# Batch 0 in two token parts, v cast by its transfer, and output stores on the ScalarE queue, in an attention + squared-ReLU kernel on one Trainium2 core

## The chip, the cores and the metric

The kernel runs on one core of one Trainium2 chip. Time is microseconds (us) of device time, a median of several executions. In this kernel TensorE (PE in the profile) does matrix multiplies, VectorE (DVE) and ScalarE (ACT) work on vectors, GpSimd (POOL) casts and issues casting transfers, SyncE (SP) issues most other transfers. With a run of the kernel before in the same call, the ratio is the mean time of one kernel's fast runs over that of the other's fast runs of the same rounds. It is therefore not quite the ratio of the medians that are quoted. The interval after a ratio is a 95% interval.

## The reference

```python
# q, k, v: (8, 8, 576, 64); beacon_k, beacon_v: (8, 8, 16, 64); all float32
k_all = concat([beacon_k, k], axis=2); v_all = concat([beacon_v, v], axis=2)
scores = q @ k_all.T / sqrt(64)              # causal, the 16 beacon keys are always seen
a = softmax(scores)
x = (a @ v_all).transpose(0, 2, 1, 3).reshape(4608, 512)
h = x @ w_in                                 # (512, 2048)
out = maximum(h, 0) ** 2 @ w_out             # (2048, 512) -> (4608, 512)
```

## The kernel before

A small list scheduler inside the kernel fixes the order of instructions on each engine. Each operation has an engine, a priority, dependencies and an *estimated* duration. The scheduler simulates time with the estimates and always issues the ready operation of the best priority. The program then holds each engine's list in that fixed order.

The chain is this. The attention of batch `b` ends with the attention-value matmuls ("av"). VectorE normalizes them into `xn`. SyncE issues five transposing transfers `xT <- xn`. The MLP goes through the tokens in chunks of 512. Its first multiply ("s1", with `w_in`), for the chunk that needs batch `b`, reads `xT`. Its second multiply gives two output units of 256 tokens for each chunk. On the same SyncE queue stand loads of q, k and v for later batches, the transposing transfers `qT` and `kT` of batch `b+2`, and the output stores.

```python
# staging load (SyncE), later cast by GpSimd
ld = add(f"ld{b}{x}{c}", "POOL" if soft else "SP", 1.3 if lo else 0.65, emit_load, prio=prio,
         take=("stg", "stg"), dma=1.1 * rows / 128, behind=load_chain[-1:] + behind, sync=sync)
# zero padding of the q/k area, once batches 1 and 2 are transposed (GpSimd)
deps = trans[NPE - 1, "q"] + trans[NPE - 1, "k"] + trans[NPE - 2, "q"] + trans[NPE - 2, "k"]
zero_ops[b] = add(f"zero{b}", "POOL", 1.0, emit, prio=10.0 * b - 1, deps=deps)
# qT / kT by transposing transfer (SyncE), batches 3 to 7
trans[b, x] = [add(f"tr{b}{x}", "SP", 3.8, emit, prio=prio, deps=deps, dma=3.2)]
# scores (TensorE): 0.17 is the fixed part of the estimate
qk = add(f"qk{p}.{n}.{i}", "PE", 0.17 + cols / 2400.0, emit_qk, prio=base + i, ...)
# xT of one 128-token tile (SyncE), batches 2 to 7; batches 0 and 1 are transposed by TensorE
deps = [norm_ops[HP * b + i, 0] for i in range(HP)] + ring_deps(tok, tok + n)
o = add(f"xt{b}.{t}", "SP", 1.32, emit, prio=-50.0 + b, deps=deps, dma=0.64 * n / 128)
# second multiply of the MLP, chunk 0: the two output units u in turn, quarter by quarter
order2 = [(u, [(ts, 4 * qd, 4 * qd + 4) for ts in range(2)], [qd]) for qd in range(4) for u in range(2)]
# output: ScalarE copies PSUM to osb, SyncE stores
ev = add(f"ev{j}.{u}", "ACT", 1.05 if ts is None else 0.6, emit_ev, prio=-15.0, ...)
st_ops[2 * j + u] = add(f"st{j}.{u}", "SP", 0.65, emit_st, prio=-20.0, deps=[ev], dma=1.4)
# filler matmuls that keep TensorE busy while the first data come
def keep_busy(slot, gap):
    for _ in range(int((gap - 0.2) / (0.07 if warm_pe else 0.11))):     # 25 the first time
        nc.tensor.matmul(ps[slot][:, 0, 0:128], filler, filler, start=True, stop=True)
# ... (cuts between all of these)
```

The softmax here doesn't subtract the row's maximum and nothing guards it: scores larger than these inputs give would overflow.

Of the kernel before, what the change touches and what calls it, by code (L numbers as in the profile page):

```python
# [187 lines left out]
def kernel(  # L188
# [11 lines left out]
    nc = tc.nc  # L200
# [9 lines left out]
    NCH = n_tokens // TCH  # L210
    NMC = d_model // 128
# [53 lines left out]
    warm_pe = []  # L265

    def keep_busy(slot, gap):
        for _ in range(int((gap - 0.2) / (0.07 if warm_pe else 0.11))):
            nc.tensor.matmul(ps[slot][:, 0, 0:128], filler, filler, start=True, stop=True)  # L269
        warm_pe.append(slot)  # L270
# [26 lines left out]
    tri_op = add("tri", "POOL", 1.0, emit_tri, prio=-150.0)  # L297
# [28 lines left out]
    SOFT_V = (1,)  # L326
    zero_ops = {}
    strided = {}

    def add_zero(b):  # L330
        def emit(e):
            nc.gpsimd.memset(qb[b % 2][:, :, NT - 1, :], 0.0)
            nc.gpsimd.memset(kb[b % 2][:, :, NT - 1, :], 0.0)
        deps = trans[NPE - 1, "q"] + trans[NPE - 1, "k"] + trans[NPE - 2, "q"] + trans[NPE - 2, "k"]
        zero_ops[b] = add(f"zero{b}", "POOL", 1.0, emit, prio=10.0 * b - 1, deps=deps)

    def add_load(b, x, c, prio, behind=[], sync=[]):
# [6 lines left out]

        soft = b in SOFT_V
        queue = nc.gpsimd if soft else nc.sync

        def emit_load(e):
            st = stg[ld.held[2]]
            insts = []  # L350
            if lo:
                insts.append(queue.dma_start(out=st[0:Nb], in_=beacon[b].transpose([1, 0, 2])))
            insts.append(queue.dma_start(out=st[lo:rows],  # L353
                                         in_=t[b, :, t0:t0 + rows - lo, :].transpose([1, 0, 2])))
            return insts

        ld = add(f"ld{b}{x}{c}", "POOL" if soft else "SP", 1.3 if lo else 0.65, emit_load,
# [14 lines left out]
        if x != "v":  # L372
            if b < NPE + 2:
                deps += [zero_ops[b]]
            else:
                deps += trans[b - 2, x]
        engs = ("POOL", "DVE") if b == 0 else ("POOL",)
        cast[b, x, c] = add(f"cast{b}{x}{c}", engs, {"DVE": 0.6, "POOL": 0.65}, emit_cast,
                            prio=prio, deps=deps, give=ld)

    def add_trans(b, x, prio):
# [11 lines left out]
        trans[b, x] = [add(f"tr{b}{x}", "SP", 3.8, emit, prio=prio, deps=deps, dma=3.2)]  # L393
# [9 lines left out]
    def add_strided(b, prio):  # L403
        loads = {}
        bk = add_beacon(b, prio)
        after = [w_ops["in", 3]] if b == 1 else [strided[b - 1][HP - 1, "q"]] if b else []
        free = trans[b - 2, "q"] + trans[b - 2, "k"] if b >= 2 else []
        trans[b, "q"], trans[b, "k"] = [], []
        step = 1 if b == 0 else 2
        for pr in range(0, HP, step):  # L410
            h = slice(2 * pr, 2 * (pr + step))
            for n, (x, t, dst) in enumerate((("k", k, ks), ("q", q, qs))):
                def emit(e, t=t, dst=dst, h=h):
                    return [nc.gpsimd.dma_start(out=dst[b % 2][:, h],
                                                in_=t[b, h].rearrange("h (p s) d -> p h s d", s=NS))]
                o = add(f"sld{b}{x}{pr}", "POOL", 0.65 * step, emit, prio=prio + pr + 0.1 * n, behind=after,
                        deps=free, dma=0.92 * step)
                for i in range(step):
                    loads[pr + i, x] = o
        strided[b] = loads  # L420
        for pr in range(HP):
# [3 lines left out]
            for part in (("k", "q") if b == 0 else ("kq",)):  # L425
                def emit_tp(e, pr=pr, h=h, boxes=boxes, part=part):
                    pp = ps[boxes[part].held[2]].bitcast(BF16)
                    if "k" in part:
                        nc.tensor.transpose(pp[:, 1, 0:Nb], bks[b % 2][:, h, :], ident[0:Nb, 0:Nb])
                    for x, half, at, t in (("k", 1, Nb, ks), ("q", 0, 0, qs)):  # L430
                        if x in part:
                            for u in range(NS):
                                for hj in range(2):
                                    nc.tensor.transpose(pp[64 * hj:64 * hj + 64, half, at + u * NP:at + (u + 1) * NP],  # L434
                                                        t[b % 2][:, 2 * pr + hj, u, :], ident[0:NP, 0:NP])

                tp = add(f"tp{b}.{pr}{part}", "PE", 0.2 + 0.35 * len(part), emit_tp,
                         prio=100.0 * (HP * b + pr) - 190 + (5 if part == "q" else 0),
                         deps=[bk, ident_op] + [loads[pr, x] for x in part] + busy, take=("ps", "tp"))

                def emit_k(e, pr=pr, boxes=boxes, part=part):
                    pp = ps[boxes[part].held[2]].bitcast(BF16)
                    copy_on(e, kT[b % 2][:, pr, 0:Nb], pp[:, 1, 0:Nb])
                    copy_on(e, kT[b % 2][:, pr, Nb:Nb + S].rearrange("p (n s) -> p n s", s=NS),
                            pp[:, 1, Nb:Nb + S].rearrange("p (s n) -> p n s", s=NS))

                def emit_q(e, pr=pr, boxes=boxes, part=part):
                    pp = ps[boxes[part].held[2]].bitcast(BF16)
                    copy_on(e, qT[b % 2][:, pr, 0:S].rearrange("p (n s) -> p n s", s=NS),
                            pp[:, 0, 0:S].rearrange("p (s n) -> p n s", s=NS))  # L450

                boxes[part] = tp
                ev = []
                if "k" in part:
                    ev.append(add(f"ek{b}.{pr}", "DVE", 0.9, emit_k, prio=-200.0, deps=[tp]))
                    trans[b, "k"].append(ev[-1])
                if "q" in part:
                    ev.append(add(f"eq{b}.{pr}", ("DVE", "ACT") if b else "ACT", 0.75, emit_q, prio=-199.0, deps=[tp]))
                    trans[b, "q"].append(ev[-1])
                add(f"tpg{b}.{pr}{part}", "-", 0.0, None, prio=0.0, deps=ev, give=tp)  # L460
# [48 lines left out]
    def add_pair(b, pr):  # L509
# [8 lines left out]
        if b < NPE:  # L518
            qk_deps = [trans[b, "k"][pr], trans[b, "q"][pr]]
        else:  # L520
            qk_deps = trans[b, "k"] + trans[b, "q"]
        take_pt = add(f"pt{p}", "-", 0.0, None, prio=100.0 * p, deps=qk_deps, take=("pt", "pt"), gate=gate)
        av_ops[p] = []
        for n, ph in enumerate(phases(b)):
            add_phase(b, pr, p, n, ph, take_pt, qk_deps, gate)

    def add_phase(b, pr, p, n, ph, take_pt, qk_deps, gate):
        base = 100.0 * p + 1000.0 * n
        exps = []
        for i in range(0, len(ph.pieces), QGROUP(b)):  # L530
# [17 lines left out]
            qk = add(f"qk{p}.{n}.{i}", "PE", 0.17 + cols / 2400.0, emit_qk, prio=base + i,  # L548
# [12 lines left out]
        def emit_mask(e):  # L561
# [5 lines left out]
            if ph.last is not None:  # L567
# [5 lines left out]
                   prio=base, deps=exps + [tri_op])  # L573
# [96 lines left out]
    def add_weights():  # L670
        for i in range(4):
            def emit(e, i=i):
                w = d_ff // 4
                return [nc.gpsimd.dma_start(
                    out=w_in_sb[:, :, i * w:(i + 1) * w],
                    in_=moe_w_in.rearrange("(m p) f -> p m f", p=128)[:, :, i * w:(i + 1) * w])]
            w_ops["in", i] = add(f"win{i}", "POOL", 1.3, emit, prio=-100 + i, sync=[v_loads[0][2]] if i == 0 else (),
                                 behind=[w_ops["in", i - 1]] if i else (), dma=3.15)
    def add_weights_out():
        for i in range(4):  # L680
# [5 lines left out]
            w_ops["out", i] = add(f"wout{i}", "POOL", 1.3, emit, prio=-90 + i, behind=[v_loads[1][4]] if i == 0 else [w_ops["out", i - 1]], dma=3.15)  # L686

    def add_chunk(j):
# [59 lines left out]
        for n, (u, work, quarters) in enumerate(order2):  # L748
            def emit_s2(e, u=u, work=work):
                o = ps[s2_first[j, u].held[2]]  # L750
                for ts, f0, f1 in work:
# [4 lines left out]
            o = add(f"s2.{j}.{u}.{n}", "PE", 1.73, emit_s2, prio=base + 100 + n,  # L756
                    deps=[x for qd in quarters for f in (2 * qd, 2 * qd + 1) for x in sq[f]]
                    + [w_ops["out", qd] for qd in quarters] + [prevs.get(u)],
                    take=("ps", "mlp") if u not in prevs else None, pe_time=1.73)
            if u not in prevs:  # L760
                s2_first[j, u] = o
            prevs[u] = o
            s2_ops[j, u] = o
        for u in range(2):
            last = j == NCH - 1 and u == 1

            for ts in (range(2) if last else [None]):
                def emit_ev(e, u=u, ts=ts):
                    o = ps[s2_first[j, u].held[2]]
                    d = osb[(2 * j + u) % 2]  # L770
                    if ts is not None:
                        o, d = o[:, ts, :], d[:, ts, :]
                    copy_on(e, d, o)

                deps = [s2_ops[j, u]]
                if (2 * j + u) >= 2:
                    deps.append(st_ops[2 * j + u - 2])
                ev = add(f"ev{j}.{u}", "ACT", 1.05 if ts is None else 0.6, emit_ev, prio=-15.0, deps=deps,
                         give=s2_first[j, u] if ts != 0 else None)

                def emit_st(e, u=u, ts=ts):
                    t0 = j * TCH + u * 256
                    d = osb[(2 * j + u) % 2]
                    if ts is None:
                        nc.sync.dma_start(out=out[t0:t0 + 256, :].rearrange("(t p) d -> p t d", p=128), in_=d)
                    else:
# [82 lines left out]
```

## Time and profile before

| | before |
|---|---|
| time, median of 3 (lowest to highest) | 355.68 us (354.88 to 358.15) |
| TensorE busy | 342.2 of 355.2 us |
| first s1 matmul | 28.2 us |
| waits of TensorE for `xT` | 3.5 us in two waits |
| granted TensorE clock, mean | 0.993 |

The page's first two parts: busy time of the engines, then the span in 40 slices, where each digit is a share in tenths and PEclk is the granted clock of TensorE.

```profile
PE 342.2 (96%) x3037; PEld 183.2 (52%) x3037; DVE 149.5 (42%) x293; ACT 189.6 (53%) x231; POOL 79.8 (22%) x130
...
PE   6999999899999999899997999999999999999994
...
PEclk9999999999999999999998999999999999999999
```

TensorE is busy 96% of the span, and 76% of the page's chain of work that ended last is on it, so it sets the time. The clock row shows one dip after the middle: the clock's records read half from 190.0 to 193.4 us. At the very start the row reads 9, but the trace has no clock record before 22.8 us. The timeline of TensorE (start, duration, what, how many) shows the real state there: twelve 96-column transposes take 0.69 us at 11.8 us, where twenty-four take 0.70 us at 36.1 us, so the clock was half there. The first s1 comes at 28.2 us.

```profile
11.79 0.69 PE L434 MATMUL ps<-ident,qk_area 96*64 96x96 bf16 x12
...
28.22 0.99 PE L713 MATMUL ps<-xT,w_in 128*128 128x240 bf16 x8
```

The waits of TensorE (who waited for what: us in total, times, longest), with one line, and the same two waits in TensorE's timeline (the brackets hold idle time and its releaser):

```profile
PE ps L713 <- DMA xT<-xn: 3.5, 2, 2.4
```

```profile
150.59 1.67 PE L713 MATMUL ps<-xT,w_in 128*128 128x512 bf16 x7 [1.13 <-DMA xT<-xn]
...
189.44 2.19 PE L713 MATMUL ps<-xT,w_in 128*128 128x256 bf16 x12 [2.42 <-DMA xT<-xn]
```

Timelines of VectorE and SyncE around the first of them: the last normalization of batch 3 (the 20th in order: batch 0 has eight, each later batch four), then what SyncE issued until `xT` of batch 3 had its turn.

```profile
132.05 0.82 DVE L601 TENSOR_TENSOR xn<-ps,rcp 128x640 bf16<-128x640 f32 x1
```

### The profile page before, as it was taken

Reading aid. Unit: us, or ns where it says so; the run is one execution under the profiler, and the core shown is the slowest. Engines: PE = TensorE matmul, PEld = TensorE weight load, DVE = VectorE, ACT = ScalarE, POOL = GpSimd, SP = SyncE. Lnnn points to the kernel's source line nnn. Section 1 sums busy time; section 2 is a strip of 40 time slices with the busy share of each in tenths; the row PEclk is TensorE's granted clock in tenths of the full one; section 3 lists DMA queues with packets and bytes.
Section 4 is the critical chain, followed back from the end, with each engine's and each line's share of the span. In section 5 each row is a group of like instructions: output and inputs, shape, how many; then the busy total and the mean of one; then the engine's idle time right before and its main releaser. Section 6 shows DMA issues by size and latency. Waiting matters only on the chain.

```text
span 355.2 us, 7320 instructions
## 1 busy us (share of the span) xinstructions
PE 342.2 (96%) x3037; PEld 183.2 (52%) x3037; DVE 149.5 (42%) x293; ACT 189.6 (53%) x231; POOL 79.8 (22%) x130
## 2 busy tenths in 40 slices
PE   6999999899999999899997999999999999999994
PEld 5569676554444444444444874444444544444441
DVE  4576784546542483236332482247224601401300
ACT  2776786867643754466443753575357305504602
POOL 8254802461422254024131330000000000000000
PEclk9999999999999999999998999999999999999999
DMA  8899999999969999789997994110211123003003
GB/s 138 145 203 216 204 205 207 244 206 214 194 118 216 225 222 234 144 154 241 229 198 138 235 222 86 61 59 18 53 59 61 28 41 118 0 2 118 0 2 118
DMA packets 137010, 49.51 MB, mean 139 GB/s; under 512 B 123344, under 2 KB 132048, under 8 KB 136976
## 3 DMA queue, kind: packets, MB, share of 16 engines
q1 hardware_dynamic: 127472, 40.09, 54.0%
q0 software_dynamic: 9504, 8.95, 15.5%
q8 instruction: 24, 0.39, 0.5%
q14 instruction: 10, 0.08, 0.1%
HBM read 37.22 MB, written 9.44 MB: 131 GB/s over the span
## 4 chain that ended last, share of the span: by engine, by line
PE 76%; DMA 11%; SPq 6%; DVE 2%; ACT 1%; issue 1%; POOL 1%; ACTq 0%; POOLq 0%
PE ps L713 31%; PE ps L753 28%; PE ps L585 7%; PE ps L541 6%; SPq L632 3%; DMA stg<-in_k_dram 3%; DMA stg<-in_q_dram 3%; DMA stg<-in_v_dram 3%; PE ps L434 2%; DMA xT<-xn 1%; DMA qk_area<-in_q_dram 1%; SPq L353 1%; PE ps L269 1%; SPq L385 1%; DVE g L738 1%
## 5 line engine op out<-in xcount | busy, mean ns | idle before, releaser
L713 PE MATMUL ps<-xT,w_in 128*128 128x512 bf16 (+3 forms) x704 | 133.5, 342 | 4.0 <-DMA xT<-xn 3.5
L753 PE MATMUL ps<-w_out,g 128*128 128x512 bf16 x576 | 132.0, 381 | 0.5 <-ACT qT L306 0.5
L555 ACT ACTIVATE pt<-ps 128x832 bf16<-128x832 f32 (+4 forms) x128 | 104.1, 865 | 45.0 <-PE ps L541 44.9
L713 PEld LDWEIGHTS <-w_in 128*128 128x128 bf16 x704 | 66.4, 98 | 60.6 <-issue 4.8
L738 DVE TENSOR_TENSOR g<-g 128x1024 bf16<-128x1024 bf16 (+2 forms) x80 | 52.9, 663 | 104.3 <-ACT g L729 104.0
L729 ACT ACTIVATE g<-ps 128x1024 bf16<-128x1024 f32 (+2 forms) x62 | 59.1, 953 | 61.6 <-PE ps L713 61.6
L753 PEld LDWEIGHTS <-g 128*128 128x128 bf16 x576 | 53.5, 98 | 67.5 <-issue 6.9
L308 POOL CAST qk_area<-stg 128x512 bf16<-128x512 f32 (+2 forms) x50 | 32.5, 658 | 55.0 <-DMA stg<-in_k_dram 32.6
L306 ACT COPY osb<-ps 128x1024 f32<-128x1024 f32 (+1 forms) x19 | 18.3, 968 | 44.0 <-PE ps L753 40.9
L585 PEld LDWEIGHTS <-pt 128*128 128x128 bf16 (+1 forms) x960 | 34.1, 99 | 8.0 <-issue 2.9
L541 PE MATMUL ps<-qT,kT 64*128 64x80 bf16 (+5 forms) x400 | 37.7, 290 | 0.0
L585 PE MATMUL ps<-vb,pt 128*128 128x65 bf16 (+1 forms) x960 | 36.3, 196 | 0.2 <-ACT pt L555 0.2
L308 POOL CAST vb<-stg 128x512 bf16<-128x512 f32 (+1 forms) x36 | 22.3, 638 | 56.4 <-DMA stg<-in_v_dram 33.2
L565 DVE TENSOR_TENSOR pt<-pt,tri 128x1024 bf16<-128x1024 bf16 (+1 forms) x36 | 24.3, 674 | 20.7 <-ACT pt L555 20.6
L601 DVE TENSOR_TENSOR xn<-ps,rcp 128x640 bf16<-128x640 f32 (+2 forms) x36 | 27.0, 750 | 1.8 <-DVE rcp L600 0.5
L600 DVE RECIPROCAL rcp<-ps 128x10 f32<-128x10 f32 (+2 forms) x36 | 7.6, 210 | 43.5 <-PE ps L585 43.5
L541 PEld LDWEIGHTS <-kT 64*128 64x128 bf16 x400 | 12.6, 96 | 20.7 <-issue 16.2
L731 DVE TENSOR_SCALAR g<-ps 128x1024 bf16<-128x1024 f32 (+2 forms) x18 | 19.0, 1054 | 8.1 <-PE ps L713 7.4
L308 DVE COPY kT<-ps 128x16 bf16<-128x16 bf16 (+1 forms) x24 | 9.7, 456 | 8.6 <-PE ps L434 8.0
L434 PE MATMUL ps<-ident,qk_area 96*64 96x96 bf16 x288 | 11.1, 233 | 2.0 <-DMA qk_area<-in_k_dram 1.1
L306 ACT COPY qT<-ps 128x576 bf16<-128x576 bf16 x12 | 7.7, 638 | 8.9 <-PE ps L434 6.2
L434 PEld LDWEIGHTS <-qk_area 96*64 96x64 bf16 x288 | 8.5, 126 | 3.6 <-DMA qk_area<-in_k_dram 1.2
(36 smaller groups left out, 71.3 us busy)
## 6 DMA issues: line engine op xcount, KB each, us to landing
out_dram<-osb SPq DMA_DIRECT2D x17, 512.0 KB, 2.8
stg<-in_v_dram SPq DMA_DIRECT2D x21, 256.0 KB, 5.6
stg<-in_q_dram SPq DMA_DIRECT2D x20, 256.0 KB, 4.8
stg<-in_k_dram SPq DMA_DIRECT2D x15, 256.0 KB, 4.6
w_in<-in_moe_w_in_dram POOLq DMA_DIRECT2D x4, 512.0 KB, 8.6
w_out<-in_moe_w_out_dram POOLq DMA_DIRECT2D x4, 512.0 KB, 10.9
stg<-in_v_dram SPq DMA_DIRECT2D x7, 224.0 KB, 4.5
qk_area<-in_k_dram POOLq DMA_DIRECT2D x4, 288.0 KB, 12.3
```

The costliest lines, as they stand in the source:

```text
L306: nc.scalar.copy(dst, src)
L308: eng[e].tensor_copy(dst, src)
L434: nc.tensor.transpose(pp[64 * hj:64 * hj + 64, half, at + u * NP:at + (u + 1) * NP], t[b % 2][:, 2 * pr + hj, u, :], ident[0:NP, 0:NP])
L541: nc.tensor.matmul(st[:, hj, at:at + t1 - t0], kT[b % 2][hp, pr, 128 * c:128 * c + 128], qT[b % 2][hp, pr, t0:t1], start=True, stop=True,)
L555: nc.scalar.activation(pt[take_pt.held[2]][:, :, off:off + width], st[:, :, 0:width], AF.Exp, bias=0.0, scale=scale)
L565: nc.vector.tensor_tensor(out=d, in0=d, in1=tri[:, m0:m0 + m, :][:, None].to_broadcast([128, 2, m, 128]), op=ALU.min)
L585: nc.tensor.matmul(a[:, hj, (t - tl[0]) * (D + 1):(t - tl[0] + 1) * (D + 1)], P[0:rr, hj, o:o + 128], vb[b % 2][0:rr, c, h, :], start=(c = ...
L601: nc.vector.tensor_tensor(out=xn[b % 2].rearrange("p t (h d) -> p h t d", d=D)[:, 2 * pr:2 * pr + 2, tl[0]:tl[0] + nt], in0=a[:, :, :, 0:D ...
L713: nc.tensor.matmul(h[:, u, lo - spans[0][0]:hi - spans[0][0]], w_in_sb[:, mc, ft * 128:(ft + 1) * 128], xT[:, mc, lo % RING:lo % RING + hi ...
L729: nc.scalar.activation(dst, h, AF.Relu, bias=0.0, scale=1.0)
L738: nc.vector.tensor_tensor(out=d, in0=d, in1=d, op=ALU.mult)
L753: nc.tensor.matmul(o[:, ts, :], G[:, fc, (2 * u + ts) * 128:(2 * u + ts + 1) * 128], w_out_sb[:, fc, :], start=(fc == 0), stop=(fc == NFT ...
```

## The change

The intent: start the MLP earlier, by bringing only 240 of batch 0's 576 tokens first, by moving the first quarter of `w_in` forward, and by casting v of batches 0 and 1 in the transfer instead of in a step of its own behind a staging buffer. More filler matmuls were meant to bring the full TensorE clock before the first transposes (in e11 below, with 50 of them, it was full from 5.1 us and the first transposes came at 5.96). The stores leave the SyncE queue, but for the last two. The last output unit is computed in halves, so that the first half is evicted under the second. Some estimates of the scheduler are changed too. The diff is cut to its core:

```diff
-    warm_pe = []
+    warm_pe, FILL = [], 50
-        for _ in range(int((gap - 0.2) / (0.07 if warm_pe else 0.11))):
+        for _ in range(FILL if not warm_pe else int((gap - 0.2) / 0.07)):
...
+    FIRST = [("kq", 0, 0), ("kq", 0, 2), "tri", ("v", 0, 1), ("kq", 1, 0), ("win", 0), ("kq", 1, 2), ("v", 2, 3, 4),
+             ("win", 1), ("win", 2), ("win", 3)]
+    SPLIT_AT = 240
...
+    def add_v(b, tiles, prio, behind=()):           # batches 0 and 1
+                insts.append(nc.gpsimd.dma_start(out=vb[b % 2][lo:rows, c, :, 0:D],
+                                                 in_=v[b, :, t0:t0 + rows - lo, :].transpose([1, 0, 2])))
...
+    PARTS = {0: [Part(0, SPLIT_AT, 0), Part(SPLIT_AT, S, 1)], 1: [Part(0, S, 1)], 2: [Part(0, S, 0)]}
...
-            qk = add(f"qk{p}.{n}.{i}", "PE", 0.17 + cols / 2400.0, emit_qk, prio=base + i,
+            qk = add(f"qk{p}.{n}.{i}", "PE", 0.2 + cols / 2400.0, emit_qk, prio=base + i,
...
-            o = add(f"s2.{j}.{u}.{n}", "PE", 1.73, emit_s2, prio=base + 100 + n,
+            o = add(f"s2.{j}.{u}.{n}", "PE", 1.75, emit_s2, prio=base + 100 + n,
...
+                    if ts is None:
+                        nc.scalar.copy(d, o)
+                        nc.scalar.dma_start(out=out[t0:t0 + 256, :].rearrange("(t p) d -> p t d", p=128), in_=d)
+                    else:                                 # LAST_U, the last unit, in halves
+                        nc.scalar.copy(d[:, ts, :], o[:, ts, :])
+                        nc.sync.dma_start(out=out[t0:t0 + 128, :], in_=d[:, ts, :])
...
-                st_ops[2 * j + u] = add(f"st{j}.{u}", "SP", 0.65, emit_st, prio=-20.0, deps=[ev], dma=1.4)
+                ev = add(f"ev{j}.{u}", "ACT", 1.15 if ts is None else 0.65, emit_ev, prio=-15.0, deps=deps, give=first)
+                st_ops[2 * j + u] = add(f"st{j}.{u}", "-", 4.0, None, prio=0.0, deps=[ev])
```

## The prediction

> **What bounds the kernel now.** The page shows PE busy 96% of 355.2 us, but not all of it useful. Summing the real matmuls at their start-to-start times late in the trace (216 ns for a 128x512, 29 ns for an attention-value matmul) against time: about 18.6 us of PE time are lost by 30 us, 2 more by 45 us, some 7 in small pieces by 140 us, 5 at 186-193 us, 4.3 after the last matmul. The rest is dense and untouched. So three places to win:
>
> 1. *Start.* The chain of waits opens with the q/k DMA (4.96 us); the first s1 matmul (L713) comes at 28.2 us. Until about 22.8 us PE runs at half speed: in the timeline twelve 96-column transposes take 0.69 us there, twenty-four take 0.70 us at 36 us. [...] the 25 first fillers last 2.85 us, then PE waits for DMA. 50 would last about 5.4 us cold[...].
> 2. *Middle.* SP issues almost without a gap from 75 to 192 us (q/k transposes 3.1-5.2 us each, five xT transposes 6.4-7 us, loads 0.5-1.1 us, stores 0.5-1.4 us), and PE waits for xT 1.13 us at 150 us and 2.42 us at 187 us; after the latter comes a half-clock stretch.
> 3. *Tail.* Two evictions (1.07 us) and two stores after the last matmul.
>
> **What the change does.** The first q/k transfers bring 240 tokens of four heads, so phase 0 of all four pairs, and xT of 240 tokens, need half of batch 0. The first w_in quarter, issued at 15.6 us before, follows the third q/k transfers, about 9-11 us by issue times of 0.64-0.75 us. In the static order s1 starts after 7.2 us of useful PE work instead of 8.9, with phase 1 of pairs 2-3 still open. I expect the first s1 at 18-22 us and the first 240 tokens' s1 done near 30 us (36 before). Limits: ScalarE has about 20 us of exps and copies for batch 0, and the bytes ahead of the last w_in quarter are the same. The casting v transfers read the same 256 B pieces; I cost them like the plain ones, about 5 us a batch. Gain 4-6 us.
>
> Stores leave SP: about 1 us each, two per batch, and no load waits behind an eviction. ScalarE pays about 0.5 us each and has room. Against it: the new PE order puts the last attention-value matmul of batches 3 to 6 only 8.5 us of PE work before the s1 that needs it (17 before). Norm 1.1, three xT transposes 3.9 and landing 2.5 make 7.5 us if SP is free. The middle waits may shrink or move: -1, between -4 and +3.
>
> Tail: the first half is evicted under the second: -0.5 us.
>
> **Prediction: 349.0 us, range 344.5 to 353.5**; faster by over 2% 0.45, within 2% 0.51, slower 0.04.
>
> **Right if:** transposes before 10 us run at full speed; first s1 before 22 us; batch-1 transposes near 31 us (36 before); no store on SP; about 4.0 us after the last matmul. **Wrong if:** the casting v transfers are slow (w_in quarters and batch 1 late), PE falls back to half clock between 7 and 20 us, or new PE waits for xT of 3 us or more appear.

Gains are 4 to 6 us at the start, 1 in the middle and 0.5 at the end, 6.5 us with the mean of the first, which from 355.7 us makes about 349. The 5.4 us for 50 fillers and the 0.5 us for a store on ScalarE were estimates; in the kernel after they are 5.52 us and 0.38 us (median of 17).

## More of the kernel before

```profile
132.11 4.24 SPq L353 DMA_DIRECT2D stg<-in_v_dram  x4
136.46 4.75 SPq L385 DMA_TRANSPOSE qT<-qk_area  x1
141.30 3.39 SPq L385 DMA_TRANSPOSE kT<-qk_area  x1
144.75 0.58 SPq L353 DMA_DIRECT2D stg<-in_v_dram  x1
145.42 6.41 SPq L632 DMA_TRANSPOSE xT<-xn  x5
```

The data for `xT` of batch 3 were ready at 132.87 us, and the transfer was issued at 145.42. For 12.6 us it stood behind other work of the same queue.

## The result

The kernel after takes 371.13 us (370.62 to 372.96, 4 runs) against 355.28 for the kernel before in the same rounds. The ratio is 1.0451, with a 95% interval of 1.0367 to 1.0535. So it is slower, and outside the predicted range of 344.5 to 353.5.

The same views of the kernel after. First the page's busy times and slices:

```profile
PE 346.1 (93%) x3116; PEld 187.5 (51%) x3152; DVE 155.8 (42%) x300; ACT 185.1 (50%) x228; POOL 84.1 (23%) x130
...
PE   8999899999999999279994999999999999999995
...
PEclk9559999999999999769998799999999999999999
```

TensorE now has a hole near 150 to 160 us and another near 200. The clock's records read half from 153.6 to 163.8 us and from 201.4 to 208.2 us, and close to the start from 10.2 to 27.3 us. The waits and the timelines name the hole:

```profile
PE ps L772 <- DMA xT<-xn: 13.5, 2, 9.0
```

```profile
149.33 1.90 PE L814 MATMUL ps<-w_out,g 128*128 128x512 bf16 x8
160.21 3.57 PE L772 MATMUL ps<-xT,w_in 128*128 128x512 bf16 x8 [8.98 <-DMA xT<-xn]
```

```profile
140.91 0.82 DVE L661 TENSOR_TENSOR xn<-ps,rcp 128x640 bf16<-128x640 f32 x1
```

```profile
141.08 5.35 SPq L352 DMA_DIRECT2D stg<-in_v_dram  x4
146.53 4.00 SPq L401 DMA_TRANSPOSE qT<-qk_area  x1
150.63 4.28 SPq L401 DMA_TRANSPOSE kT<-qk_area  x1
155.00 6.45 SPq L692 DMA_TRANSPOSE xT<-xn  x5
```

`xT` of batch 3 was ready to be issued at 141.73 us and was issued at 155.00, 13.3 us later, behind four v loads and the two transposing transfers of batch 5. The queue time is about the same as before (12.6 us). What differs is how much work TensorE had in between. In the static order of before, 17 us of TensorE work lie between the last attention-value matmul and the s1 that needs it. In the order of after it is 8.5 us for most batches and about 10 us for batch 3 (weighed as in the sum below).

The start, in the timeline of TensorE:

```profile
6.62 0.62 PE L461 MATMUL ps<-ident,qk_area 40*64 40x40 bf16 x24
...
9.84 0.59 PE L461 MATMUL ps<-ident,qk_area 40*64 40x40 bf16 x24
10.37 0.49 PE L601 MATMUL ps<-qT,kT 64*128 64x240 bf16 x4
```

Four score matmuls with 240 columns take 0.33 us at 8.2 us and 0.49 us from 10.4 us on. The clock's records say the same: full from 6.8 to 10.2 us, then half until 27.3.

To follow the lost time I made a sum of my own from the trace (not a view of the profile). It is the elapsed time less the dense duration of all matmuls whose weight loads have begun. The dense durations are those seen late in the trace (216 ns for a 128x512, in proportion to columns for narrower ones, 30 ns for an attention-value matmul, 22 ns for a transpose). Fillers count as lost.

| lost TensorE time up to | before | after |
|---|---|---|
| 20 us | 15.4 | 14.0 |
| 35 us | 19.2 | 19.4 |
| 140 us | 28.7 | 29.9 |
| 170 us | 31.2 | 41.5 |
| 210 us | 37.2 | 50.4 |
| 300 us | 40.4 | 54.7 |

The spans differ by 16.0 us (371.2 less 355.2). Of this, 1.2 came by 140 us, 9.1 between 140 and 170, 2.9 between 170 and 210, 1.1 from 210 to 300. The 96 extra transposes cost 2.1 (96 times 22 ns), and the end after the last weight load is 0.3 shorter (4.75 against 5.09 us). The terms add to 16 within rounding.

### The profile page after: what moved, and what is told of

Read it like the earlier page. It is cut to its first block, busy times and chain, and to the rows that moved or that the text cites. A ratio compares the mean times of both kernels' runs of the same rounds, so it can differ in the third digit from the quotient of the medians.

```text
span 371.2 us, 7429 instructions
## 1 busy us (share of the span) xinstructions
PE 346.1 (93%) x3116; PEld 187.5 (51%) x3152; DVE 155.8 (42%) x300; ACT 185.1 (50%) x228; POOL 84.1 (23%) x130
## 4 chain that ended last, share of the span: by engine, by line
PE 75%; DMA 9%; SPq 5%; POOL 4%; DVE 3%; issue 2%; ACT 1%; POOLq 0%; DVEq 0%; ACTq 0%
PE ps L772 30%; PE ps L814 30%; PE ps L645 7%; PE ps L601 6%; DMA stg<-in_q_dram 3%; DMA stg<-in_k_dram 3%; DMA qk_area<-in_k_dram 3%; SPq L692 2%; PE ps L461 1%; SPq L401 1%; POOL vb L310 1%; SPq L352 1%; POOL qk_area L435 1%; DVE g L790 1%; DMA stg<-in_v_dram 1%
## 5 line engine op out<-in xcount | busy, mean ns | idle before, releaser
L772 PE MATMUL ps<-xT,w_in 128*128 128x512 bf16 (+3 forms) x687 | 137.1, 348 | 15.8 <-DMA xT<-xn 13.5
L788 ACT ACTIVATE g<-ps 128x1024 bf16<-128x1024 f32 (+2 forms) x54 | 53.1, 983 | 75.0 <-PE ps L772 74.6
L601 PE MATMUL ps<-qT,kT 64*128 64x80 bf16 (+7 forms) x400 | 37.1, 288 | 0.8 <-DVE kT L310 0.6
L625 DVE TENSOR_TENSOR pt<-pt,tri 128x1024 bf16<-128x1024 bf16 (+1 forms) x36 | 24.5, 681 | 28.2 <-ACT pt L615 28.2
L310 POOL CAST vb<-stg 128x512 bf16<-128x512 f32 (+1 forms) x30 | 19.2, 661 | 72.9 <-DMA stg<-in_v_dram 51.6
L835 ACT COPY osb<-ps 128x1024 f32<-128x1024 f32 x17 | 17.2, 1013 | 36.5 <-PE ps L814 36.5
L790 DVE TENSOR_SCALAR g<-ps 128x1024 bf16<-128x1024 f32 (+2 forms) x26 | 26.0, 1002 | 15.4 <-PE ps L772 13.6
L308 ACT COPY qT<-ps 128x576 bf16<-128x576 bf16 (+2 forms) x16 | 8.2, 519 | 14.7 <-PE ps L461 10.0
L310 DVE COPY kT<-ps 128x16 bf16<-128x16 bf16 (+3 forms) x28 | 10.4, 413 | 10.2 <-PE ps L461 9.3
L461 PE MATMUL ps<-ident,qk_area 96*64 96x96 bf16 (+2 forms) x384 | 11.7, 209 | 0.8 <-DMA qk_area<-in_k_dram 0.8
L461 PEld LDWEIGHTS <-qk_area 96*64 96x64 bf16 (+2 forms) x384 | 9.5, 120 | 2.4 <-DMA qk_area<-in_k_dram 1.3
## 6 DMA issues: line engine op xcount, KB each, us to landing
w_in<-in_moe_w_in_dram POOLq DMA_DIRECT2D x4, 512.0 KB, 12.2
qk_area<-in_k_dram POOLq DMA_DIRECT2D x4, 288.0 KB, 12.6
```

The lines of the kernel that those rows point to most:

```text
L310: eng[e].tensor_copy(dst, src)
L461: nc.tensor.transpose(pp[64 * hj:64 * hj + 64, half, at + u * n:at + (u + 1) * n], t[pt_.i][0:n, 2 * pr + hj, u, :], ident[0:n, 0:n])
L601: nc.tensor.matmul(st[:, hj, at:at + t1 - t0], kT[b % 2][hp, pr, 128 * c:128 * c + 128], qT[b % 2][hp, pr, t0:t1], start=True, stop=True,)
L625: nc.vector.tensor_tensor(out=d, in0=d, in1=tri[:, m0:m0 + m, :][:, None].to_broadcast([128, 2, m, 128]), op=ALU.min)
L772: nc.tensor.matmul(h[:, u, lo - spans[0][0]:hi - spans[0][0]], w_in_sb[:, mc, ft * 128:(ft + 1) * 128], xT[:, mc, lo % RING:lo % RING + hi ...
L788: nc.scalar.activation(dst, h, AF.Relu, bias=0.0, scale=1.0)
```

## The experiments

### First group: the estimate, and a late memset

The static order flips with one number. With the estimate 0.2 for a score group, the scheduler interleaves both output units of chunk 0, which hold two of the four PSUM slots. The last q/k transposes of batch 2 then come late. So does the GpSimd memset of the padding that waits for them: it starts at 80.3 us in the kernel after and at 67.9 us before. Meanwhile SyncE issues nothing for 14.1 us (68.7 to 82.8 in the kernel after): its next load waits for GpSimd's first cast to empty a staging buffer, and that cast comes behind the memset. My first theory was that this late memset delays all later loads, and with them `xT`. The rival was that the start or the stores cause the loss.

**e1: the kernel after with the old estimate.**

```diff
-            qk = add(f"qk{p}.{n}.{i}", "PE", 0.2 + cols / 2400.0, emit_qk, prio=base + i,
+            qk = add(f"qk{p}.{n}.{i}", "PE", 0.17 + cols / 2400.0, emit_qk, prio=base + i,
```

> The changed kernel, with one number put back: the scheduler's estimate of a q-k matmul group, 0.2 to 0.17 us. No instruction is added or removed; only the static order changes (last q/k transposes of batch 2 earlier; the two output units of chunk 0 no longer hold two of four PSUM slots at once). Theory A (order: late batch-2 transposes -> late padding memset -> casts -> SP loads stop at 72-83 us -> xT of batch 3 late): padding memset near 70 us, no SP hole, PE wait for xT at 150-160 us under 2 us, 354-358 us. Rival B (casting v transfers, stores on ScalarE, or the two-part q/k loads cost it): stays at 368 us or more.

Measured: 357.69 us (before: 355.61; ratio 1.0064, 1.0032 to 1.0096). No wait for `xT` is left, and the memset starts at 71.4 us. One constant that describes nothing of the hardware is worth 13.4 us here (371.13 less 357.69, from different calls), through the order alone.

**e2: the kernel before with the new estimate**, the same line the other way round (0.17 to 0.2).

> The kernel before, with that one number changed the other way: 0.17 to 0.2 us. None of the change's loads, casts, stores or fillers. Theory A: the padding memset moves from 68 us to about 80 us, SP stops loading there, PE waits 6 us or more for xT of batch 3, 366-373 us. Rival B: 354-357 us as before.

Measured: 361.27 us (355.61; 1.0155, 1.0096 to 1.0215). That is only about half of the expected loss. TensorE waited 6.8 us for `xT` in all. In this order SyncE issued `xT` of batch 3 directly behind `qT` at 145.51, ahead of `kT`. The memset was at 76.7 us, so it was late too, but the result was half as bad. The memset alone cannot be the cause.

**e3: the kernel before with the memset made long** (13 times the same memset for batch 3).

```diff
+            for _ in range(13 if b == NPE else 1):
-            nc.gpsimd.memset(qb[b % 2][:, :, NT - 1, :], 0.0)
-            nc.gpsimd.memset(kb[b % 2][:, :, NT - 1, :], 0.0)
+                nc.gpsimd.memset(qb[b % 2][:, :, NT - 1, :], 0.0)
+                nc.gpsimd.memset(kb[b % 2][:, :, NT - 1, :], 0.0)
```

> The kernel before, its static order untouched, but the padding memset of batch 3 on GpSimd is repeated 13 times (about 12 us more; result unchanged). It delays the casts of batch 3 alone. Theory A in its strict form (the hole in SP's loads alone is enough): SP stops loading for 10-12 us near 70-82 us, PE waits for xT near 150 us grow from 1 to 6-11 us, 362-370 us. Rival A2 (what matters is the PE order, which puts the s1 of a chunk only 8.5 us behind the attention it needs; the hole is absorbed): within 2 us of before.

Measured: 364.29 us (355.61; 1.0246, 1.0211 to 1.0282). The time falls in the expected range, but for another reason. The hole on SyncE is there, but the loss came at 90 to 100 us, where TensorE waited for `kT` of batch 3. The wait for `xT` of batch 3 is 1.2 us, as before (1.1). The two lines are from the timeline of SyncE and from the groups of TensorE (busy, mean ns, idle before and its releaser):

```profile
68.50 14.29 SPq L354 DMA_DIRECT2D stg<-in_k_dram  x3
```

```profile
L542 PE MATMUL ps<-qT,kT 64*128 64x80 bf16 (+5 forms) x400 | 37.9, 291 | 6.6 <-DMA kT<-qk_area 6.6
```

So the theory of the memset fell: a late memset costs time where batch 3 starts, not where the kernel after loses it. A time inside the expected range did not make the theory right.

**e4: the kernel after, chunk 0's output units one after the other.**

```diff
-... for qd in range(4) for u in range(2)]
+... for u in range(2) for qd in range(4)]
```

> The changed kernel, with the output matmuls of chunk 0 ordered unit by unit instead of quarter by quarter, so that one PSUM slot, not two, is held while they run; estimates as changed. If the PSUM slots are why the batch-2 transposes come late: padding memset near 70 us, no SP hole, 354-359 us, like the first run of this set. If not: 368 us or more.

Measured: 357.77 us (355.61; 1.0060, 1.0023 to 1.0098). That is the same as e1 by another route. With the estimate still at 0.2, taking the interleaving away is enough to take the loss away. So it is the order that costs the time.

### Second group: the parts of the change one by one

**e6: the kernel before with its stores on the ScalarE queue.**

```diff
+                    if ts is None:
+                        nc.scalar.dma_start(out=out[t0:t0 + 256, :].rearrange("(t p) d -> p t d", p=128), in_=d)
...
+                if ts is None:
+                    st_ops[2 * j + u] = add(f"st{j}.{u}", "-", 4.0, None, prio=0.0, deps=[ev])
+                    continue
```

> The kernel before, with the stores issued on ScalarE's queue as in the change, nothing else (the batch-2 transposes keep their places; the order further on shifts, the distance from attention to s1 grows). Theory A: no harm from the stores themselves: 351-356 us, xT of batch 4 issued before 184 us. Rival B2 (stores on ScalarE hold up exps and cost time): 358 us or more.

Measured: 354.03 us (355.79; 0.9956, 0.9871 to 1.0041). The scheduler now leaves 27 us of TensorE work between attention and s1, and the waits for `xT` are gone. But 5.6 us are lost at 60 to 70 us (the kernel before loses 2.7 there). The timeline of ScalarE shows it: the first output copy ends at 62.30, its store is issued only at 64.21, and the exponentials that TensorE needs come after it.

```profile
61.29 1.01 ACT L306 COPY osb<-ps 128x1024 f32<-128x1024 f32 x1 [0.60 <-PE ps L753]
64.21 0.42 ACTq L776 DMA_DIRECT2D out_dram<-osb  x1
64.73 1.70 ACT L555 ACTIVATE pt<-ps 128x928 bf16<-128x928 f32 x2 [2.43 <-DMA stg<-in_k_dram]
```

The trace also tells why the store was issued 1.9 us after its copy. ScalarE stood at a semaphore (a counter, raised here by the landing of a transfer) that the store shares with a load of k on SyncE, the one that the bracket of the last line names. That load was issued at 59.10 and landed at 64.13 us, 0.08 us before the store. In e14 and e15 it is the same (landed 63.40 and 63.94, store 63.48 and 64.02). In e1 the load that shares the store's semaphore had landed at 65.08 us, before the copy ended at 70.63, and the store follows the copy by 0.03 us. The stores' own time did not shrink on the other queue: 2.8 us from issue to landing in the kernel before and in e6, 3.6 in the kernel after.

**e7: e1 with the stores on SyncE**, and **e8: e1 with four more fillers at each place** (204 fillers in the trace against 76 in e1; the text says about 80 more).

```diff
-        for _ in range(FILL if not warm_pe else int((gap - 0.2) / 0.07)):
+        for _ in range(FILL if not warm_pe else 4 + max(0, int((gap - 0.2) / 0.07))):
```

> The first run of the first set (estimate 0.17), with the stores back on SP. It differs from that run by the stores and the order that follows. If the stores on ScalarE are neutral or better: 356-360 us. If they cost: 352-355 us.

> The first run of the first set (estimate 0.17), with four more fillers at each place in batch 0 (about 80 more). Theory C (the start gains nothing because the clock falls back to half at 10.3 us until 27.3 us; sixteen s1 take 3.38 us and twenty-four attention-value matmuls 1.49 us there): clock full before 22 us, time lost on PE at 35 us 2 us less, 354-356 us. Rival (start is limited by transfers and ScalarE): clock may come, lost time at 35 us within 0.7 us, 357-359 us.

Measured: e7 358.23 us (355.79; 1.0093, 1.0019 to 1.0167), with a wait of 3.6 us for `xT` at 187 us. That is the first case of the expectation: on ScalarE the stores are no worse than on SyncE. e8 360.07 us (1.0131, 1.0057 to 1.0206), above both of its ranges. In e8 the clock stays full from 6.6 to 74.9 us, yet the first s1 comes at 26.6 us, because the fillers themselves stand in TensorE's list. So e8 bears on the fall of the clock at 10.2 us in the kernel after. Idle time does not stand before that fall: TensorE has no gap of 0.2 us from 6.5 to 11.9 us. And e1, where the clock falls too (at 10.3 us), differs from e8 only by fillers put between the small transposes. From 6.8 to 10.2 us the kernel after does 24-fold groups of 40-column transposes of 0.55 to 0.62 us each, with some 0.5 us of fillers and score matmuls between them. In e8 most groups are of twelve (0.36 us), with four fillers (0.40 us) behind most of them. Why the clock falls without these fillers, and whether the kind of the instruction or its small size counts, no run separates.

**e9 and e10: stores on ScalarE except those of chunk 0**, in the kernel before and in e1. These were meant to keep e6's gain without its loss.

> The kernel before, its PE order unchanged, with the stores of chunks 1 and later on ScalarE and those of chunk 0 left on SP. In the run with all stores on ScalarE the first eviction and store stood between exps at 62-65 us and PE lost 5.6 us there; but the xT wait at 187 us was gone. Theory D (the store move helps SP later and hurts only where ScalarE feeds PE alone): both losses gone, no PE wait for xT over 1 us, 349-353 us. If the store move has no effect of its own: 354-357 us.

> The same stores in the changed kernel with the estimate 0.17. Against the run just before it differs by the start (two token parts, casting v, earlier w_in, fillers) and the tail. If the start gains as predicted (4-6 us): 345-348 us. Theory E (the start gains nothing: 96 more transposes are 2.1 us of PE, the last w_in quarter lands later): 351-355 us, 1-3 us above the run just before it.

Measured: e9 361.08 us (356.63; 1.0124, 1.0089 to 1.0159), e10 361.63 (1.0130, 1.0089 to 1.0170). Both missed. In e9 TensorE waits for `xT` of batch 3 again, which was issued at 147.64 behind `qT` and `kT`. In e10 it waits 6.1 us for that of batch 4. Every shuffle of other things moved the place of `xT` on the queue.

**e11: the kernel before with 50 first fillers, nothing else.**

```diff
-        for _ in range(int((gap - 0.2) / (0.07 if warm_pe else 0.11))):
+        for _ in range(50 if not warm_pe else int((gap - 0.2) / 0.07)):
```

> The kernel before with 50 first fillers, nothing else; same order. If the half clock until 22.8 us is what costs the start there, and 50 fillers lift it: first s1 before 25.5 us, 351-354 us. If they lift it [...] as in the changed kernel (6.8 to 10.2 us): 354-357 us.

Measured: 353.63 us (356.63; 0.9929, 0.9891 to 0.9966), as the first case of the expectation had it. The clock is full from 5.1 us, the first s1 comes at 23.2 us, and by 30 us 5.1 us are gained (own sum: 14.1 lost against 19.2). Then 4.3 of them are lost at one place. `xT` of batch 3 was ready at 128.15 (its normalization started at 127.33 and took 0.82) and was issued at 142.79, 14.6 us later:

```profile
134.32 3.99 SPq L385 DMA_TRANSPOSE qT<-qk_area  x1
138.40 3.66 SPq L385 DMA_TRANSPOSE kT<-qk_area  x1
142.12 0.58 SPq L353 DMA_DIRECT2D stg<-in_v_dram  x1
142.79 7.48 SPq L632 DMA_TRANSPOSE xT<-xn  x5
```

**e12: the kernel before with v of batches 0 and 1 cast by the transfer, `w_in` directly behind, chunk 0 unit by unit.**

> The kernel before with v of batches 0 and 1 cast by the transfer, and w_in following directly without a wait; chunk 0 unit by unit so that the order stays the good one. If casting transfers cost as plain ones: last w_in quarter lands by 29.5 us, 352-356 us. If 128-byte writes are slower (1.7-2.1 ns apiece in the changed kernel's trace against some 1.1 for plain 256-byte pieces): last w_in quarter lands after 30.5 us, 356-359 us.

Measured: 355.97 us (356.63; 0.9976, 0.9937 to 1.0014), so the same. The last `w_in` quarter landed at 28.3 us (29.5 before), so the casting transfers did not make `w_in` late here. Its start was 2.7 us better by 35 us (16.5 lost), and its waits for `xT` were 3.2 us.

### Third group: the place of xT on the SyncE queue

**e5: the kernel after; `qT` and `kT` of batch b wait for `xT` of batch b-2.**

```diff
         deps += [o for p in range(HP * (b - 2), HP * (b - 1)) for o in qk_ops[p]]
+        if b - 2 >= NXPE:
+            deps += [xt_ops[b - 2, t] for t in range(NT)]
```

> The changed kernel with one more dependency for the scheduler: the q and k transposes of batch b (on SP) wait for the xT transposes of batch b-2, so SP issues xT first. PE's order is the same as in the changed kernel. Theory A (SP reaches xT late, 4.3 us of it because two transposes stand ahead, the rest from the hole): PE waits for xT of batches 3 and 4 fall from 9 and 3.5 us to 1-5 us, 360-366 us; the padding memset stays at 80 us. If it is the attention of the batch itself that is late, not SP's queue: 369 us or more.

Measured: 369.43 us (355.79; 1.0396, 1.0313 to 1.0480), a miss. The edit took `qT` and `kT` away from in front of `xT`, but the scheduler filled the space with loads of batch 6. `xT` was issued at 149.48, 8.7 us after its normalization, and the five took 9.31 us instead of 6.45. TensorE waited 7.2 us. At this point the matter looked open: either the normalization comes too late with 8.5 us of distance, or the queue is still wrong.

**e16: the kernel after with `xT` of batch b-2 strictly first**, by order of issue, with no load of batch b+1 in between (the v loads of batch b itself still stand in front). Two edits, which are also those of e13 to e18 where "strict" is named (there on the kernel before, with `trans[b, x]` for `trans[b, x, 0]`; e15 has none of it):

```diff
-        trans[b, x, 0] = [add(f"tr{b}{x}", "SP", 3.8, emit, prio=prio, deps=deps, dma=3.2)]
+        trans[b, x, 0] = [add(f"tr{b}{x}", "SP", 3.8, emit, prio=prio, deps=deps, dma=3.2,
+                              behind=[xt_ops[b - 2, t] for t in range(NT)] if b - 2 >= NXPE else [])]
...
                 sync = [w_ops["out", 3]]
+            elif b > NPE and n == 0:
+                behind = trans[b - 1, "q", 0] + trans[b - 1, "k", 0]
             add_load(b, x, c, lp + 0.1 * n, behind, sync)
```

> The kernel after, estimates and PE order as there (8.5 us of PE work between attention and its s1), with the xT transposes of batch b directly ahead of qT and kT of batch b+2 and no later load between; in e5 two to four loads had slipped in front of xT, which was issued at 149.5 with its last normalization done at 147.4. Theory (the late place on the queue made the 9 us wait, the short distance only makes 3): the wait for xT of batch 3 falls from 9.0 us to 2 to 4.5 us, each of batches 4 to 6 waits up to 4 us, time 362 to 367. Rival (the queue is moved for nothing: the late normalization alone sets it): wait of batch 3 7 us or more, time 368 to 372.

Measured: 358.90 us (355.90; 1.0075, 1.0016 to 1.0134), 12.2 us less than the kernel after (371.13; another call). The instructions are the same, and so is their order on TensorE, VectorE and ScalarE. Only SyncE's order differs, and with it ten casts on GpSimd that follow the loads. The time is below the range that the theory gave. The wait of batch 3 fell from 9.0 to 3.5 us, and batches 4 to 6 do not wait. (The text takes a normalization at 147.4 us for that of batch 3. Counting the normalizations shows that batch 3's was done at 141.5 in this run. Likewise it was at 128.2 in e11, not 137.4.) `xT` now comes 6.7 us after it, behind v loads only:

```profile
142.02 6.10 SPq L352 DMA_DIRECT2D stg<-in_v_dram  x5
148.22 7.30 SPq L693 DMA_TRANSPOSE xT<-xn  x5
155.62 2.96 SPq L401 DMA_TRANSPOSE qT<-qk_area  x1
```

```profile
154.52 3.57 PE L773 MATMUL ps<-xT,w_in 128*128 128x512 bf16 x8 [3.50 <-DMA xT<-xn]
```

**e13: the kernel before with 50 fillers and the strict order.**

> The kernel before with 50 first fillers (as e11), and on the SyncE queue the five xT transposes of batch b put directly ahead of the qT and kT transposes of batch b+2, with no load of later batches between. PE order unchanged. In e11 the start gained 5.1 us by 30 us (own sum), but TensorE stood 4.3 us at 144.7 to 149.0 for xT of batch 3, which was issued at 142.8 behind qT and kT (134.3 to 142.1) although its last normalization was done at 137.4. Theory (what a head start gains is taken back by the place of xT in the SyncE queue): xT of batch 3 is issued at 137.4 to 139, no wait for xT at 145, no half clock at 148, time 347.5 to 351.5. Rival (the head start is taken back wherever the next wait stands, since another chain sets the pace): a wait of 3 us or more appears between 100 and 215 us in another place, time 352.5 to 355.

Measured: **347.38 us** (347.09 to 348.32, 6 runs; before 355.90; 0.9758, 0.9730 to 0.9787). This beats both kernels and lies just below the range of the theory. `xT` of batch 3 was issued at 135.61 us, still 7.1 us after its normalization, but with 17 us of TensorE work in between no wait came of it. The rival of a loss elsewhere is out: TensorE's waits hold nothing over 1.1 us, and the clock is full from 7.0 us to the last matmul. Its views, SyncE, TensorE, then the two longest waits of TensorE:

```profile
130.49 5.02 SPq L353 DMA_DIRECT2D stg<-in_v_dram  x5
135.61 6.46 SPq L633 DMA_TRANSPOSE xT<-xn  x5
142.16 3.75 SPq L385 DMA_TRANSPOSE qT<-qk_area  x1
```

```profile
143.43 1.67 PE L754 MATMUL ps<-w_out,g 128*128 128x512 bf16 x7 [0.16 <-issue]
144.94 1.89 PE L714 MATMUL ps<-xT,w_in 128*128 128x512 bf16 x8
```

```profile
PE ps L269 <- DVE warm L277: 1.1, 1, 1.1
PE ps L754 <- issue: 1.0, 6, 0.2
```

**e14 and e15: 50 fillers with the stores on ScalarE, with and without the strict order.**

> As e13, with the output stores on the ScalarE queue. The scheduler then places the attention of batches 3 to 6 about 27 us of PE work before the s1 that needs it (17 in the kernel before). In e6 the stores on ScalarE took away the wait for xT at 187 us but cost 5.6 us at 60 to 70 us. Theory (the two are separate and add): no waits for xT over 1 us, a loss of 4 to 6 us at 60 to 70, time 348 to 353. Rival (the loss at 60 to 70 in e6 came from its late start): with the earlier start that loss is under 2 us, time 345 to 348.

> As e14 without the strict order of xT on the SyncE queue, so e6 plus 50 fillers. Theory (with 27 us of PE work between attention and its s1 the order on the queue does not matter): within 1 us of e14. Rival (order on the queue matters still): a wait for xT of 2 us or more, and 2 us or more slower than e14.

Measured: e14 352.77 us (355.90; 0.9913, 0.9878 to 0.9947), e15 353.51 (0.9931, 0.9888 to 0.9974). They are within 1 us of each other, as the theory had it: with 27 us between attention and s1 the queue does not matter. The loss at 60 to 70 us is back in e14. Against e13, e14 takes 5.4 us more; the own sum puts 3.5 us of it at 60 to 70 us and 1.4 at 70 to 75, in the half clock that follows (six 128x512 matmuls of the second multiply take 2.77 us from 68.70 us; seven take 1.67 us at 143.43 in e13).

**e17: the strict order alone**, and **e18: e13 with the estimate 0.2.**

> The kernel before with the strict order of xT on the SyncE queue alone, 25 first fillers as there. In e13 (50 fillers and strict order) no wait for xT is left; e11 (50 fillers alone) took off 2.3 us at most. Theory (two independent gains: about 5 us at the start, and in the middle the waits of 1.13 and 2.42 us with the half clock after the second): no wait for xT, start lost as before (about 19 us by 30 us), time 350 to 353. Rival (the order alone does the most, the fillers matter little): 347 to 349.5; or (the two waits of before were hidden by something else): 354 or more.

> e13 with the one estimate 0.17 set to 0.2, which leaves 8.5 to 10.2 us of PE work between the attention of batch 3 to 6 and the s1 that needs it, in place of 17. In e16 xT of batch 3 was issued 6.7 us after its normalization and TensorE waited 3.5 us. Theory (the distance is worth what the remaining chain of normalization, 7 us on the queue, transposes and landing exceeds it): a wait for xT of 2.5 to 5 us at batch 3 and half clock after it, time 351 to 356. Rival (with the queue in order the distance does not matter): no wait above 1 us, time under 349.5.

Measured: e17 351.63 us (356.00; 0.9874, 0.9834 to 0.9914). The start loses 19.2 us by 30 us as before, and no wait for `xT` is left. So the gains about add: 3.0 us from fillers (e11, against its own before), 4.4 from the order (e17), 8.5 from both (e13). That is 1.1 more than the sum, which is within the noise (each ratio is known to about 1.0 to 1.4 us). e18: 348.18 us (0.9791, 0.9756 to 0.9826). A wait of 2.6 us for `xT` of batch 3 is there, as the theory had it, but no half clock follows (the next eight 128x512 matmuls take 1.89 us, where in e16 they took 3.57) and the time is the rival's. The length of a wait alone does not tell whether half clock follows: this one was 2.56 us, while the wait of 2.42 us in the kernel before was followed by half clock from 190.0 to 193.4 us, and two waits of 1.22 and 1.15 us in e1 by half clock from 75.1 to 78.5. What decides it, these runs do not show. With the queue in order, the estimate that was worth 13.4 us in the kernel after costs about 0.8 us (348.18 less 347.38, different calls, so not more than a hint).

| lost TensorE time up to | before | e17 | e13 | e18 | e16 | after |
|---|---|---|---|---|---|---|
| 35 us | 19.2 | 19.2 | 14.9 | 15.2 | 19.4 | 19.4 |
| 140 us | 28.7 | 28.8 | 24.2 | 23.6 | 29.7 | 29.9 |
| 170 us | 31.2 | 30.2 | 25.9 | 27.7 | 37.1 | 41.5 |
| 210 us | 37.2 | 32.2 | 28.2 | 29.8 | 39.3 | 50.4 |

The row at 35 us is the start, the steps between 140 and 210 us are the waits for `xT` with their half clock. That e16 still loses 11 us more than e13 by 210 us splits into the start (4.5), the stretch up to 140 us (1.0, by the differences of the rows) and the rest at 140 to 170 us, where its wait of 3.5 us was followed by 6.8 us of half clock.

The traces of all these runs show that the wait needs both terms, the stay in the queue and a short distance. In e1 and e15 `xT` of batch 3 stood longer in the queue than in the kernel after (15.8 and 17.0 us), and TensorE did not wait, since 27 us of work lay between. With about 10 us of work it waited 9.0 us after 13.3 us in the queue (after), 3.5 after 6.7 (e16) and 2.6 after 6.0 (e18).

## Why the prediction was wrong

- **What bounds the kernel: right.** TensorE, busy 96% of the span before, bounds it; the places of loss were the start, the middle and the end.
- **The middle: wrong, and this is the step that failed.** The prediction said: "Norm 1.1, three xT transposes 3.9 and landing 2.5 make 7.5 us if SP is free. The middle waits may shrink or move: -1, between -4 and +3." It saw the 8.5 us of TensorE work in the new order, and 7.5 is less than 8.5. But SyncE was not free. In the kernel after, `xT` of batch 3 stood 13.3 us in the queue after its data were ready, a term that the sum did not have. The rest of the sum was about right: the normalization took 1.1 us, and the third `xT` landed 5.1 us after the first was issued (6.4 in the sum). With the queue that makes 19.4 us against about 10 us of work. It cost 13.5 us of waits, with half clock at each (10.2 and 6.8 us of it), and the own sum puts about 12 us more loss at 140 to 210 us than in the kernel before. e16 took 12.2 us off by the order on the queue alone. The same term was in the trace of before, 12.6 us, mostly hidden by the 17 us of distance there. The prediction's own list of what would make it wrong names "new PE waits for xT of 3 us or more"; that is what came.
- **The changed estimates: overlooked.** The prediction reads the distance of 8.5 us from the new order but not its cause. The cause was the estimate 0.17 to 0.2: put back, it gives 27 us for batch 3 (e1), and in the kernel before it cuts 17 us to about 10 (e2). The two token parts are in e1 as well and did not cause it.
- **The start: wrong in size.** "Gain 4-6 us" was 1.9 us at 25 us (16.4 lost against 18.3 in the own sum) and nothing at 35. The transposes before 10 us did run at full speed (clock records full from 6.8 to 10.2 us) and the first s1 came at 22.8 us (18 to 22 expected, 28.2 before). But then the clock was half from 10.2 to 27.3 us, and the 64th s1 matmul came at 37.1 us, later than before (35.7). The batch-1 transposes came at 38.2 us instead of 31. The median time from issue to landing of a `w_in` quarter rose from 8.6 to 12.2 us. In e8, with more fillers between the small transposes, the clock stayed full (6.6 to 74.9 us); how the remaining loss divides between clock and late `w_in` stays open. The prediction named this danger as well ("PE falls back to half clock between 7 and 20 us").
- **Fillers: borne out in the runs with the old start.** With 50 of them and the unsplit batch 0 (e11) the clock was full from 5.1 us, ahead of the first transposes at 5.96, where it was full from 22.8 us in the kernel before; 5.1 us were gained by 30 us. That 25 fillers always leave it half so long is not shown: e6, with 25, was granted 0.75 at 5 to 10 us, 0.91 at 10 to 15 and full clock after. In the kernel after the clock was lost again at 10.2 us, among the small transposes of the first part; no run has the two parts alone.
- **Stores: half right.** SyncE was relieved (only the two half stores of the last unit are left there) and the scheduler could keep more distance (27 us in e6). What went wrong in e6 and e14, around the first output unit, was not a lack of room: ScalarE stood idle for 1.9 and 1.5 us, at the semaphore that the store shared with a load of SyncE.
- **Casting v transfers: costed too low, without a loss shown.** Their 128-byte packets took 32 ns (median) in the kernel after and 46 ns in e12, where the plain 256-byte packets took 18 ns. e12, which has them without the split, is the same as before in time. What they cost in the kernel after is not separated.
- **Extra transposes: missing in the sum.** 96 of them, 2.1 us.
- **The end: right.** -0.5 us predicted, -0.3 measured.

## What to carry to other kernels

For a transfer on the critical path, subtract the time its data were ready from the time of its issue: the difference is its stay in the queue, which no single line of the profile shows and which other work may be hiding. In these runs it cost time only where the work in between was shorter than the whole chain. Put urgent transfers ahead of long ones by an explicit order rather than by priorities and estimates; here that gave 4.4 us, and 8.5 us together with 50 filler matmuls. When a diff changes a constant of a scheduler, compare the distances in the resulting order first, before costing the rest.
